# Copying reciprocal rows between SBUF partitions with four transfers instead of through a DRAM row

## The chip, the cores and the metric

The kernel runs on one core of a Trainium2 chip. The metric is the device time of one execution, in microseconds (us). The kernel before takes 621.2 us (median of 3, 618.96 to 623.64).

The engines are named as the profile names them: PE (TensorE matmul), PEld (its weight loads), DVE (VectorE), ACT (ScalarE), POOL (GpSimd), SP (SyncE). SPq and ACTq are the issues of transfers by SP and ACT.

## The reference

Causal attention with a decay by forget gates, followed by a feed-forward layer with SiLU:

```python
# q, k, v: (8, 8, 576, 64) f32; f: (8, 8, 576); w_in: (512, 2048); w_out: (2048, 512)
scores = q @ k^T / 8 + (cum_i - cum_j)        # cum = cumsum(log(clip(f, 1e-4, 1)))
attn   = softmax(scores with causal mask)
x      = (attn @ v), heads side by side       # (4608, 512)
h      = x @ w_in
out    = (h * sigmoid(h)) @ w_out             # (4608, 512) f32
```

## The kernel before

A "unit" is one pair of heads of one batch: 32 units, each with S = 576 queries. Per unit, PE transposes q and k (tp, copied by DVE to qkT), makes transposed scores (sc), ACT takes the exponential (u), and DVE masks it. Two sums over the keys follow: the numerator (nm, 64 partitions for each head) and the denominator (dn). To save PE and DVE time, the denominator is computed for two units (four heads) at once, 32 partitions for each head, and one reciprocal on DVE serves all four. The numerator needs the reciprocal on 64 partitions for each head, so rows have to be copied across partitions. That copy is the subject:

```python
    def den(qd):                      # for units 2*qd and 2*qd + 1
        dn = psc.tile([P, 1024], FP32, name="dn", tag="sc")
        ...                           # matmuls: head j on partitions 32j to 32j+31, all 32 rows equal
        rec = recp.tile([P, S], FP32, name="rec", tag="rec")
        nc.vector.reciprocal(out=rec[:, :], in_=dn[:, 0:S])
        row = drow.tile([4, S], FP32, name="row", tag="row")          # in DRAM
        nc.sync.dma_start(out=row[:, :], in_=rec[0:P:32, :])
        for m in range(2):
            rb = rbp.tile([P, S], FP32, name="rb", tag="rb")
            nc.sync.dma_start(
                out=rb[:, :],
                in_=row[2 * m : 2 * m + 2, None, :].to_broadcast([2, D, S]),
            )
            recs[2 * qd + m] = rb

    def num(n):
        ...                           # matmuls: nm, 64 partitions for each head
        rb = recs.pop(n)
        nc.vector.tensor_tensor(
            out=xT[:, p, b * S : (b + 1) * S], in0=nm[:, 0:S], in1=rb[:, :], op=ALU.mult
        )
```

The feed-forward layer is cut into tasks of four matmuls of 512 columns, hp (first layer; ACT tanh and DVE gt follow) and po (second layer), and `fill(k)` puts k of them between the attention steps to keep PE busy. `finished(n)` allows the hp tasks that need the outputs up to unit n:

```python
    for n in range(NU):
        scores(n, 0); fill(1); ...; scores(n, 1); fill(1); scores(n, 2); fill(2)
        if n % 2 == 0 and n >= 2:
            den(n // 2 - 1)
            fill(2)
        if n % 2 == 1 and n >= 3:
            num(n - 3)
            fill(1)
            num(n - 2)
            finished(n - 2)
            fill(1)
        if n + 1 < NU:
            transposes(n + 1)
        fill(2)
```

While DVE waits for rb before it can write xT, it does nothing else in these traces (the timeline below shows it idle for 5.15 and 5.26 us before two xT). The qkT copy and the gt work that come after xT on DVE wait too, and so does PE: tp, sc, dn and nm share two PSUM buffers, and the one that holds nm is free again only when xT has been written (PE's tp waits 45.4 us for xT in all, below). The pairs of units alternate: around one reciprocal the fills are mostly po, around the next mostly hp (the prediction calls them po half and hp half).

The softmax here doesn't subtract the row's maximum and nothing guards it: scores larger than these inputs give would overflow.

## Time and profile before

| | before |
|---|---|
| time, median | 621.2 us |
| span of the profiled run | 618.5 us |
| PE busy, and idle (span less busy) | 421.5, 197.0 us |
| DVE, ACT busy | 232.1, 203.4 us |
| mean granted PE clock | 0.885 |

No engine is busy all the time. First, of the page's part 4, the chain of work that ended last, by engine and by line:

```profile
DMA 46%; PE 22%; DVE 12%; issue 10%; ACT 4%; POOL 3%; SPq 1%; DVEq 0%; POOLq 0%; ACTq 0%
DMA rb<-row 37%; PE po L371 9%; PE hp L344 9%; DVE rec L294 7%; DMA row<-rec 5%; ACT u L241 3%; DMA qkb<-in_q_dram 3%; POOL qkb L71 2%; PE sc L234 2%; DVE gt L353 2%; PE tp L197 1%; SPq L299 1%; DVE xT L326 1%; DMA qkb<-in_k_dram 1%; PE dn 
```

Second, the waits: who waited for what, in total us, how often, and the longest.

```profile
DVE xT L326 <- DMA rb<-row: 191.5, 32, 26.1
...
PE hp L344 <- DVE xT L326: 68.4, 16, 5.9
...
PE sc L234 <- DVE qkT L203: 49.2, 19, 6.4
...
PE tp L197 <- DVE xT L326: 45.4, 7, 25.3
```

Every one of the 32 units waits for its rb on DVE, and PE's three largest waits are for things that DVE writes. Third, the timeline of one such stall (each `...` marks lines left out; start in us, duration, engine, line, operation, output<-inputs, count, and in brackets the idle time before it and what ended it):

```profile
220.45 3.76 DVE L294 RECIPROCAL rec<-dn 128x576 f32<-128x576 f32 x1 [0.98 <-PE dn L286]
220.56 1.67 PE L371 MATMUL po<-w_out_bf,gt 128*128 128x512 bf16 x7 [0.16 <-issue]
...
224.24 0.54 SPq L296 DMA_DIRECT2D row<-rec  x1
...
225.99 1.10 SPq L299 DMA_DIRECT2D rb<-row  x2
...
231.67 0.86 PE L314 MATMUL nm<-u,vp 128*64 128x512 bf16 x16
...
232.60 0.60 PE L344 MATMUL hp<-xT,w_in_bf 128*128 128x512 bf16 x2
...
234.96 0.76 DVE L326 TENSOR_TENSOR xT<-nm,rb 128x576 bf16<-128x576 f32 x1 [5.15 <-DMA rb<-row]
235.77 0.38 PE L344 MATMUL hp<-xT,w_in_bf 128*128 128x512 bf16 x1 [2.56 <-DVE xT L326]
...
240.97 0.76 DVE L326 TENSOR_TENSOR xT<-nm,rb 128x576 bf16<-128x576 f32 x1 [5.26 <-DMA rb<-row]
241.79 0.59 PE L344 MATMUL hp<-xT,w_in_bf 128*128 128x512 bf16 x1 [5.64 <-DVE xT L326]
...
242.16 1.50 PE L197 MATMUL tp<-ident_bf,qkb 128*128 128x128 bf16 x10
...
244.00 3.19 PE L344 MATMUL hp<-xT,w_in_bf 128*128 128x512 bf16 x7 [0.34 <-issue]
```

The reciprocal ends at 224.2. From the issue of the row to that of the first rb it takes 1.75 us. Both rb transfers are issued by 227.1, but DVE can use the first at 234.96 and the second only at 240.97. PE was through with num at 232.7. After the stall PE is slow as well: 7 hp matmuls take 3.19 us, where 7 po matmuls took 1.67 us at 220.56.

Last, one stretch of the view by windows, in which almost nothing but rb moves; the last two columns are the DMA share and GB/s:

```profile
core 0: us, PE busy (x) PEld busy (x) DVE busy (x) ACT busy (x) POOL busy (x), PEclk, DMA share, GB/s
460.50:473.00 12.50, 9.96 (x82) 4.62 (x80) 4.78 (x9) 4.71 (x9) 0.00 (x0) 1.00 0.13 47
```

A share of 0.13 of sixteen engines comes to 2.1: rb takes as much engine time as two of the sixteen have.

### The profile page before, as it was taken

To read this page: it belongs to the slowest core of one execution; us is meant where nothing else is said; L and a number is where in the kernel's file an instruction comes from. 1 tells how busy PE (TensorE), PEld (TensorE's weight loads), DVE (VectorE), ACT (ScalarE), POOL (GpSimd) and SP (SyncE) were. 2 spreads that over 40 slices of the span, in tenths; PEclk is the share of its full clock that TensorE was granted. 3 is DMA by queue.
4 is the path that set the end of the run, shared out by engine and by line. 5 is a ranking of instruction groups with operands and counts; after the bars stand their busy time and mean duration, and the time that the engine had idled before them with its cause. 6 is when DMAs were issued, how large, how long until landed. Compare 5 with 4: busy or idle time off the path is not lost.

```text
span 618.5 us, 7337 instructions
## 1 busy us (share of the span) xinstructions
PE 421.5 (68%) x2966; PEld 184.2 (30%) x3013; DVE 232.1 (38%) x337; ACT 203.4 (33%) x312; POOL 118.2 (19%) x154
## 2 busy tenths in 40 slices
PE   0461033977678594868596785859486948939997
PEld 0231021432233141323232242424232413414443
DVE  1440041743246132724165133713272328406430
ACT  2240021532245131712254233613172317105431
POOL 8738213130305003410305011500000000000000
PEclk9999997887969596977879697979799969978999
DMA  9999943291239114561329110911101110120011
GB/s 148 132 164 191 126 97 83 38 100 29 95 72 89 35 55 121 39 74 39 100 50 97 36 69 22 85 36 57 46 13 45 50 41 13 52 83 1 17 52 68
DMA packets 126705, 42.71 MB, mean 69 GB/s; under 512 B 113744, under 2 KB 117840, under 8 KB 126672
## 3 DMA queue, kind: packets, MB, share of 16 engines
q0 software_dynamic: 79392, 13.64, 28.8%
q1 hardware_dynamic: 47280, 28.61, 16.8%
q8 instruction: 23, 0.38, 0.3%
q14 instruction: 10, 0.08, 0.1%
HBM read 46.28 MB, written 9.58 MB: 90 GB/s over the span
## 4 chain that ended last, share of the span: by engine, by line
DMA 46%; PE 22%; DVE 12%; issue 10%; ACT 4%; POOL 3%; SPq 1%; DVEq 0%; POOLq 0%; ACTq 0%
DMA rb<-row 37%; PE po L371 9%; PE hp L344 9%; DVE rec L294 7%; DMA row<-rec 5%; ACT u L241 3%; DMA qkb<-in_q_dram 3%; POOL qkb L71 2%; PE sc L234 2%; DVE gt L353 2%; PE tp L197 1%; SPq L299 1%; DVE xT L326 1%; DMA qkb<-in_k_dram 1%; PE dn L286 1%
## 5 line engine op out<-in xcount | busy, mean ns | idle before, releaser
L344 PE MATMUL hp<-xT,w_in_bf 128*128 128x512 bf16 x553 | 151.9, 407 | 71.5 <-DVE xT L326 68.4
L241 ACT ACTIVATE u<-sc 128x1024 bf16<-128x1024 f32 x96 | 97.3, 1027 | 182.2 <-PE sc L234 139.7
L371 PE MATMUL po<-w_out_bf,gt 128*128 128x512 bf16 x552 | 149.5, 412 | 3.6 <-issue 2.9
L352 ACT ACTIVATE th<-hp 128x512 bf16<-128x512 f32 x144 | 86.9, 604 | 162.7 <-PE hp L344 157.2
L353 DVE SCALAR_TENSOR_TENSOR gt<-th,hp 128x512 bf16<-128x512 bf16 x144 | 95.8, 681 | 66.9 <-ACT th L352 66.9
L326 DVE TENSOR_TENSOR xT<-nm,rb 128x576 bf16<-128x576 f32 x32 | 24.3, 758 | 191.5 <-DMA rb<-row 191.5
L344 PEld LDWEIGHTS <-w_in_bf 128*128 128x128 bf16 x576 | 52.6, 102 | 97.9 <-issue 53.4
L234 PE MATMUL sc<-qkT 64*128 64x512 bf16 (+4 forms) x320 | 44.1, 351 | 53.4 <-DVE qkT L203 49.2
L371 PEld LDWEIGHTS <-gt 128*128 128x128 bf16 x576 | 53.5, 103 | 68.1 <-issue 20.0
L197 PE MATMUL tp<-ident_bf,qkb 128*128 128x128 bf16 (+1 forms) x320 | 40.3, 259 | 45.7 <-DVE xT L326 45.4
L294 DVE RECIPROCAL rec<-dn 128x576 f32<-128x576 f32 x16 | 60.1, 3754 | 6.3 <-PE dn L286 6.3
L197 PEld LDWEIGHTS <-qkb 128*128 128x128 bf16 (+1 forms) x320 | 27.5, 113 | 106.2 <-issue 97.3
L71 POOL DMA_DIRECT2D qkb<-in_q_dram x45 | 38.9, 864 | 97.9 <-PE tp L197 91.3
L254 DVE TENSOR_TENSOR u<-u,mask 128x768 bf16<-128x768 bf16 x32 | 17.9, 558 | 77.7 <-ACT u L241 77.7
L380 ACT ACTIVATE osb<-po 128x512 f32<-128x512 f32 x36 | 21.5, 597 | 63.3 <-PE po L371 46.4
L234 PEld LDWEIGHTS <-qkT 64*128 64x128 bf16 x320 | 12.0, 101 | 99.2 <-DVE qkT L203 60.9
L71 POOL DMA_DIRECT2D qkb<-in_k_dram x45 | 38.5, 855 | 11.4 <-DMA w_in_bf<-in_moe_w_in_dram 5.0
L314 PE MATMUL nm<-u,vp 128*64 128x64 bf16 (+4 forms) x512 | 30.0, 264 | 0.2
L203 DVE COPY qkT<-tp 128x1152 bf16<-128x1152 bf16 x32 | 23.6, 738 | 9.5 <-PE tp L197 9.5
L314 PEld LDWEIGHTS <-vp 128*64 128x64 bf16 x512 | 20.1, 117 | 17.9 <-issue 12.7
L286 PE MATMUL dn<-u,w_bf 128*32 128x64 bf16 (+4 forms) x512 | 14.8, 261 | 0.2
L286 PEld LDWEIGHTS <-w_bf 128*32 128x32 bf16 (+1 forms) x576 | 10.9, 100 | 10.8 <-issue 6.4
(73 smaller groups left out, 106.5 us busy)
## 6 DMA issues: line engine op xcount, KB each, us to landing
rb<-row SPq DMA_DIRECT2D x32, 288.0 KB
out_dram<-osb SPq DMA_DIRECT2D x36, 256.0 KB
qkb<-in_q_dram POOLq DMA_DIRECT2D x28, 128.0 KB, 6.6
qkb<-in_k_dram POOLq DMA_DIRECT2D x28, 128.0 KB, 12.9
w_in_bf<-in_moe_w_in_dram POOLq DMA_DIRECT2D x4, 512.0 KB, 10.3
w_out_bf<-in_moe_w_out_dram POOLq DMA_DIRECT2D x4, 512.0 KB, 10.7
qkb<-in_q_dram POOLq DMA_DIRECT2D x15, 64.0 KB, 6.0
qkb<-in_k_dram POOLq DMA_DIRECT2D x15, 64.0 KB, 6.6
```

Of the source, the lines that this page charges most:

```text
L71: nc.gpsimd.dma_start(out=qkb[b][:n, i, c, h0 * D : h1 * D].rearrange("p (h d) -> p h d", d=D), in_=src[b, h0:h1, c * P : c * P + n, :].re ...
L197: nc.tensor.transpose(tp[:, i, c * P : c * P + nk], src[:nk, i, c, p * P : (p + 1) * P], ident_bf[:nk, :nk],)
L234: nc.tensor.matmul(sc[:, i, col : col + q1 - q0], lhsT=t[r, 1, kb * P : (kb + 1) * P], rhs=t[r, 0, q0:q1], start=True, stop=True,)
L241: nc.scalar.activation(out=u[:, :, c * 512 : (c + 1) * 512], in_=sc[:, :, :], func=ACT.Exp, scale=scale)
L286: nc.tensor.matmul(dn[32 * j : 32 * j + 32, q0:q1], lhsT=w_bf[r, kb, bh : bh + 1].to_broadcast([nk, 32]), rhs=rhs, start=(kb == 0), stop=( ...
L294: nc.vector.reciprocal(out=rec[:, :], in_=dn[:, 0:S])
L314: nc.tensor.matmul(nm[i * D : (i + 1) * D, q0:q1], lhsT=v_t[r, p, :] if kb == NM else vp[:, kb, 2 * p + i, :], rhs=(ut[r, :] if kb == NM e ...
L326: nc.vector.tensor_tensor(out=xT[:, p, b * S : (b + 1) * S], in0=nm[:, 0:S], in1=rb[:, :], op=ALU.mult)
L344: nc.tensor.matmul(hp[:, :], lhsT=w_in_bf[:, cc, fc * P : (fc + 1) * P], rhs=xT[:, cc, t0 : t0 + TG], start=(cc == 0), stop=(cc == NCC - 1),)
L352: nc.scalar.activation(out=th[:, :], in_=hp[:, :], func=ACT.Tanh, scale=0.5)
L353: nc.vector.scalar_tensor_tensor(out=gt[:, fc, :], in0=th[:, :], scalar=1.0, in1=hp[:, :], op0=ALU.add, op1=ALU.mult,)
L371: nc.tensor.matmul(po[:, :], lhsT=gt[:, fc, tb * P : (tb + 1) * P], rhs=w_out_bf[:, fc, :], start=(fc == 0), stop=(fc == NFC - 1),)
```

## The change

The intent is to drop the DRAM row and to copy the reciprocals inside SBUF: the 32 equal rows of a head go twice, to fill its 64 partitions. The call of `finished` moves behind the next fill. The diff is complete:

```diff
-    drow = ctx.enter_context(tc.tile_pool(name="drow", bufs=3, space=bass.MemoryType.DRAM))
@@ den
         nc.vector.reciprocal(out=rec[:, :], in_=dn[:, 0:S])
-        row = drow.tile([4, S], FP32, name="row", tag="row")
-        nc.sync.dma_start(out=row[:, :], in_=rec[0:P:32, :])
         for m in range(2):
             rb = rbp.tile([P, S], FP32, name="rb", tag="rb")
-            nc.sync.dma_start(
-                out=rb[:, :],
-                in_=row[2 * m : 2 * m + 2, None, :].to_broadcast([2, D, S]),
-            )
+            for i in range(2):
+                j = 2 * m + i
+                for h in range(2):
+                    nc.sync.dma_start(
+                        out=rb[i * D + 32 * h : i * D + 32 * h + 32, :],
+                        in_=rec[32 * j : 32 * j + 32, :],
+                    )
             recs[2 * qd + m] = rb
@@ main loop
             num(n - 2)
+            fill(1)
             finished(n - 2)
-            fill(1)
```

## The prediction

> **What bounds the kernel now.** No engine: the page shows PE busy 421.5 of 618.5 us, DVE 232.1, ACT 203.4. The chain of waits gives 36.8% to the transfer rb<-row and 5.1% to row<-rec. In the waits, DVE xT sits 191.5 us (32 times, every unit) for rb<-row; behind it PE hp waits 68.4 us, tp 45.4 us, and sc 49.2 us (for qkT[...]). The timeline of one pair of units: rec 220.45 to 224.2, row issued 224.24, both rb 225.99 to 227.1, xT at 234.96 and 240.97 (rb lands 9 and 15 us after issue); PE had finished num at 232.6. After the stall PE runs cold: 7 hp in 3.19 us against 8 in 1.90.
>
> **Why rb is slow.** The source of rb<-row has an outermost dimension of 2. [...] The trace agrees: with only rb in flight (460.5 to 473 us), the DMA share is 0.13 (2/16) at 47 GB/s.
>
> **The change.** It removes row<-rec (1.7 to 3 us to landing) and replaces each rb by four transfers of 32 partitions[...]. Eight issues at about 0.55 us (one SP issue as measured) cost 4.4 us of SP per pair instead of 1.6. Estimate, with 1.7 us landing as for row<-rec: first rb ready 3.9 us after rec ends, second 6.1 us (before: 10.7 and 16.8). PE reaches num about 5.5 us (po half) or 6.7 us (hp half) after rec ends and ends the second num 3 us later, so both waits vanish. Moving `finished` keeps the fill after num off the xT being written; under 1 us per pair once rb is early.
>
> **Sum.** Between the recs a pair takes 33 us; PE work from warm stretches (hp x8 1.9, tp 0.98, dn 0.94, nm 1.0) is 21 to 22 us, plus about 1.6 us in the hp-heavy half, where qkT waits behind rec and gt on DVE. I take 23 us: 12 pairs save about 120 us. Start (up to 108 us): the first two rb land at 73 and 80 us because they share saturated DMA queues (queue share over 1.3 until 73 us), and the next ones stop PE from 97 to 107; I expect 20 to 25 us saved, as the loads remain. End: last rb at 555.9 instead of about 545, and 8 us of cold clock: 13 us. Together 155 to 165 us: about 456 us.
>
> **What would show it.** rb in the waits of DVE xT falls from 191.5 to under 25 us, nearly all in the first 80 us; DMA gone from the chain, PE (hp, po) the largest share; pair period 22 to 24 us; PEclk near 1.0 in the middle; PE busy about 370 us; DVE work (gt behind rec) the new largest wait.
>
> **What would make it wrong.** [...] v loads and output stores ahead of rb issues could hold them (out stores wait 251.7 us for osb already). Issue may cost more than 0.55 us. The order on DVE, ACT, SP may be built differently. The start may save nothing. DVE may stop PE more at the denser pace.
>
> Predicted 456 us, 8 in 10 between 436 and 490; faster by over 2%: 0.97, same 0.02, slower 0.01.

Two were about the order of work on DVE and SP; what a trace shows of it is that in after the copies are issued from 48.5 us on, behind a v load issued at 48.1, though the first reciprocal ended at 42.0. The "8 us of cold clock" are in the trace of before: from 556.7 to 565.0 us the granted PE clock is 0.68, then 1.00.

## The result, and the profile after

The kernel after takes 457.38 us (median of 4, 456.47 to 457.59); before in the same comparison 622.07 (4 runs). The ratio is 0.7354, 95% interval 0.7323 to 0.7386. Ratios here and below are the mean time of one kernel's fast runs over that of the other's of the same rounds, so not quite the ratio of the medians.

The chain, and the waits that answer to those of before (most lines have moved by one; L326 is still xT):

```profile
PE 48%; DMA 13%; issue 12%; DVE 11%; ACT 7%; SPq 4%; POOL 4%; DVEq 0%; POOLq 0%; ACTq 0%
PE po L371 27%; PE hp L344 10%; DMA rb<-rec 8%; ACT u L240 6%; DVE gt L353 5%; PE nm L314 4%; DMA qkb<-in_q_dram 4%; SPq L299 4%; PE sc L233 3%; DVE rec L293 3%; POOL qkb L70 3%; PE tp L196 3%; PE dn L285 1%; DMA qkb<-in_k_dram 1%; ACT th L
```

```profile
PE sc L233 <- DVE qkT L202: 26.9, 16, 4.0
...
DVE xT L326 <- DMA rb<-rec: 23.9, 8, 13.8
...
PE tp L196 <- DVE xT L326: 13.1, 1, 13.1
...
PE hp L344 <- DVE xT L326: 0.8, 1, 0.8
```

DVE's wait for rb falls from 191.5 to 23.9 us, of which 13.8 are one wait in the start. PE's wait for xT falls from 68.4 + 45.4 to 13.9 us, again nearly all in the start. The same stretch of work in the timeline:

```profile
250.29 3.76 DVE L293 RECIPROCAL rec<-dn 128x576 f32<-128x576 f32 x1 [0.83 <-PE dn L285]
...
254.07 5.18 SPq L299 DMA_DIRECT2D rb<-rec  x8
...
259.60 0.86 PE L314 MATMUL nm<-u,vp 128*64 128x512 bf16 x16
...
260.65 0.76 DVE L326 TENSOR_TENSOR xT<-nm,rb 128x576 bf16<-128x576 f32 x1 [0.79 <-PE nm L314]
261.51 0.86 PE L314 MATMUL nm<-u,vp 128*64 128x512 bf16 x16
...
262.56 0.76 DVE L326 TENSOR_TENSOR xT<-nm,rb 128x576 bf16<-128x576 f32 x1 [1.15 <-PE nm L314]
263.32 0.98 PE L196 MATMUL tp<-ident_bf,qkb 128*128 128x128 bf16 x10
...
264.46 1.67 PE L344 MATMUL hp<-xT,w_in_bf 128*128 128x512 bf16 x7 [0.16 <-issue]
```

Eight issues take 5.2 us, and now xT waits for PE (nm), not for a transfer. PE goes on without a gap and at its full pace (7 hp in 1.67 us). The view of the tile rb gives the median time from issue to landing of a copy as 2.1 us (1.9 to 10.9).

Where the 164.2 us of span went is read by stage. A stage ends where the same PE instruction starts in both traces (tp of the seventh unit; tp of the 31st), or with the last xT. The first column is the stretch, the second its length, then busy us of PE and others, PE clock, DMA share (it adds up the time of all packets, so it can exceed 1), GB/s:

```profile
0.00:108.10 108.10, 31.89 (x284) 17.49 (x286) 26.21 (x47) 21.85 (x28) 55.08 (x80) 0.97 1.13 134
108.10:504.10 396.00, 292.79 (x2127) 123.43 (x2161) 160.24 (x228) 140.55 (x216) 63.11 (x74) 0.85 0.38 60
504.10:556.70 52.60, 39.69 (x310) 18.07 (x315) 23.62 (x30) 17.15 (x28) 0.00 (x0) 0.89 0.12 43
556.70:618.50 61.80, 57.14 (x248) 25.25 (x252) 22.00 (x32) 23.90 (x40) 0.00 (x0) 0.94 0.09 35
```

```profile
0.00:80.00 80.00, 30.39 (x281) 16.94 (x281) 26.39 (x46) 21.96 (x28) 50.01 (x74) 1.00 1.45 164
80.00:354.00 274.00, 257.30 (x2127) 115.80 (x2162) 160.67 (x229) 138.80 (x215) 68.45 (x80) 1.00 0.64 91
354.00:395.20 41.20, 38.88 (x315) 17.90 (x319) 23.66 (x30) 17.74 (x29) 0.00 (x0) 1.00 0.20 57
395.20:454.30 59.10, 54.50 (x248) 24.65 (x252) 22.02 (x32) 23.91 (x40) 0.00 (x0) 0.98 0.11 39
```

The start gives 28.1 us, the twelve pairs of units in the middle 122.0 (396.0 to 274.0, that is 33.0 to 22.8 us per pair), the last pairs 11.4, the end 2.7. Seen from PE: the busy time of the same instructions falls from 421.5 to 381.1 us, 40.4 us, and idle time from 197.0 to 73.2 us, 123.8 us. The stalls thus cost about a third again of their length in slow matmuls after them. In the stall shown above, after the idle time of 5.64 us, 7 hp took 3.19 us and not 1.67, and PE was slow from 241.79 to about 247.7, some 5.9 us.

### The profile page after: what moved, and what is told of

Same layout as the page of the kernel before. It is cut to its first block, busy times and chain, and to the rows that moved or that the text cites. A ratio compares the mean times of both kernels' runs of the same rounds, so it can differ in the third digit from the quotient of the medians.

```text
span 454.3 us, 7436 instructions
## 1 busy us (share of the span) xinstructions
PE 381.1 (84%) x2966; PEld 175.3 (39%) x3013; DVE 232.7 (51%) x337; ACT 202.4 (45%) x312; POOL 118.5 (26%) x154
## 4 chain that ended last, share of the span: by engine, by line
PE 48%; DMA 13%; issue 12%; DVE 11%; ACT 7%; SPq 4%; POOL 4%; DVEq 0%; POOLq 0%; ACTq 0%
PE po L371 27%; PE hp L344 10%; DMA rb<-rec 8%; ACT u L240 6%; DVE gt L353 5%; PE nm L314 4%; DMA qkb<-in_q_dram 4%; SPq L299 4%; PE sc L233 3%; DVE rec L293 3%; POOL qkb L70 3%; PE tp L196 3%; PE dn L285 1%; DMA qkb<-in_k_dram 1%; ACT th L352 1%
## 5 line engine op out<-in xcount | busy, mean ns | idle before, releaser
L344 PE MATMUL hp<-xT,w_in_bf 128*128 128x512 bf16 x551 | 136.8, 380 | 2.9 <-issue 1.1
L371 PE MATMUL po<-w_out_bf,gt 128*128 128x512 bf16 x554 | 134.3, 380 | 2.6 <-issue 2.1
L371 PEld LDWEIGHTS <-gt 128*128 128x128 bf16 x576 | 50.8, 98 | 59.0 <-issue 5.2
L344 PEld LDWEIGHTS <-w_in_bf 128*128 128x128 bf16 x576 | 49.9, 98 | 58.9 <-issue 7.5
L233 PE MATMUL sc<-qkT 64*128 64x512 bf16 (+4 forms) x320 | 40.6, 325 | 31.9 <-DVE qkT L202 26.9
L326 DVE TENSOR_TENSOR xT<-nm,rb 128x576 bf16<-128x576 f32 x32 | 24.2, 756 | 45.0 <-DMA rb<-rec 23.9
L196 PE MATMUL tp<-ident_bf,qkb 128*128 128x128 bf16 (+1 forms) x320 | 34.5, 231 | 13.3 <-DVE xT L326 13.1
L196 PEld LDWEIGHTS <-qkb 128*128 128x128 bf16 (+1 forms) x320 | 24.3, 102 | 28.8 <-issue 15.4
L285 PEld LDWEIGHTS <-w_bf 128*32 128x32 bf16 (+1 forms) x576 | 10.9, 100 | 10.8 <-issue 6.4
## 6 DMA issues: line engine op xcount, KB each, us to landing
w_out_bf<-in_moe_w_out_dram POOLq DMA_DIRECT2D x4, 512.0 KB, 11.4
```

What stands on the lines that cost most here:

```text
L196: nc.tensor.transpose(tp[:, i, c * P : c * P + nk], src[:nk, i, c, p * P : (p + 1) * P], ident_bf[:nk, :nk],)
L233: nc.tensor.matmul(sc[:, i, col : col + q1 - q0], lhsT=t[r, 1, kb * P : (kb + 1) * P], rhs=t[r, 0, q0:q1], start=True, stop=True,)
L326: nc.vector.tensor_tensor(out=xT[:, p, b * S : (b + 1) * S], in0=nm[:, 0:S], in1=rb[:, :], op=ALU.mult)
L344: nc.tensor.matmul(hp[:, :], lhsT=w_in_bf[:, cc, fc * P : (fc + 1) * P], rhs=xT[:, cc, t0 : t0 + TG], start=(cc == 0), stop=(cc == NCC - 1),)
L371: nc.tensor.matmul(po[:, :], lhsT=gt[:, fc, tb * P : (tb + 1) * P], rhs=w_out_bf[:, fc, :], start=(fc == 0), stop=(fc == NFC - 1),)
```

## The experiments

Three theories stood at the start. **A**: an rb transfer runs on about 2 of the 16 engines (0.13 of them by its DMA share), because its source has an outermost (slowest) dimension of 2; the number of engines is the whole cost. **B**: the trip through DRAM is the cost, and SBUF as source is what helps. **C**: PE stalls because the fill after num needs the xT just written, and the move of `finished` is what helps. That the count goes with the dimension was the assumption at this point, which the runs test. Eleven kernels were run; all are correct. The traces show no engine count of a transfer, only DMA share and landing time; where a share was read it stands beside the count.

### finished_only: before, with finished moved

```diff
             num(n - 2)
+            fill(1)
             finished(n - 2)
-            fill(1)
```

> The kernel before with only the later call of finished. Theory A (the transfer rb<-row runs on 2 of 16 engines and that is the whole cost): 612 to 624 us, within 2% of before, DVE xT still waits about 190 us for rb<-row. Rival C (PE stalls because the fill after num needs the xT just written): under 600 us.

Measured: 613.15 us, ratio 0.9856 (0.9828 to 0.9883).

```profile
DVE xT L326 <- DMA rb<-row: 187.7, 30, 25.5
PE tp L197 <- DVE xT L326: 64.0, 14, 25.0
PE hp L344 <- DVE xT L326: 35.9, 9, 5.4
```

The wait for rb stays (187.7 us). PE waits 32.5 us less in hp and 18.6 us more in tp: most of the stall is only met at another instruction. C is worth 8 us in the kernel before and does not explain the change.

### copies_only: after, with finished back in its old place

```diff
             num(n - 2)
-            fill(1)
             finished(n - 2)
+            fill(1)
```

> The kernel after with finished back in its old place: the four transfers alone. Theory A: 455 to 468 us, PE hp waits for DVE xT some 0 to 1 us per pair of units, up to 10 us in all. Rival C: at least 490 us.

Measured: 457.48 us, ratio 0.7369 (0.7342 to 0.7396), against 0.7354 for the whole change. The copies alone are the whole effect. The 8 us of the move are gone here, as it hides part of a stall that no longer exists (PE hp waits for xT for 1.4 us in all).

### dram_k16, dram_k8, dram_k4: the DRAM row kept, the outermost dimension larger

Each head's row is written several times (32 equal rows are there to take from), so that a transfer's source can have 4, 8 or 16 rows outermost. There are still one write and two read transfers for each pair of units. For 16, with finished moved as in after:

```diff
-        row = drow.tile([4, S], FP32, name="row", tag="row")
-        nc.sync.dma_start(out=row[:, :], in_=rec[0:P:32, :])
+        row = drow.tile([32, S], FP32, name="row", tag="row")
+        nc.sync.dma_start(out=row[:, :], in_=rec[0:P:4, :])
@@
-                in_=row[2 * m : 2 * m + 2, None, :].to_broadcast([2, D, S]),
+                in_=row[16 * m : 16 * m + 16, None, :].to_broadcast([16, 8, S]),
```

(For 8: 16 rows, rec[0:P:8], [8, 16, S]. For 4: 8 rows, rec[0:P:16], [4, 32, S].)

> The DRAM row is kept, but written with each head's row 8 times (32 rows) so that the source of each rb transfer has an outermost dimension of 16; finished moved as in after; still one write and two reads per pair of units. Theory A (engine count): 452 to 470 us, DVE xT waits under 35 us for rb. Rival B (the trip through DRAM is the cost): above 560 us, xT still waits over 120 us.

> As the run before, with each head's row twice (8 rows), outermost dimension 4. Theory A: each rb takes about 3.5 us instead of 7, so the second rb lands about 11 us after rec ends, some 2 us after PE needs it: 465 to 510 us. Rival B: above 560 us, equal to the variant of 16 within 2%.

> DRAM row with each head's row 4 times, outermost dimension 8. Theory A: rb transfers take half of the time of the variant of 4 (501 us), both land before PE has finished num: 461 to 475 us, close to the variant of 16 (462.4).

| outermost dimension | 2 (before) | 2 (finished_only) | 4 | 8 | 16 | after (SBUF) |
|---|---|---|---|---|---|---|
| median, us | 621.2 | 613.15 | 501.01 | 471.51 | 462.39 | 457.38 |
| ratio to before | 1 | 0.9856 | 0.8061 | 0.7578 | 0.7443 | 0.7354 |
| DVE xT waits for rb, us | 191.5 | 187.7 | 99.2 | 44.5 | 29.2 | 23.9 |

All three lie in A's range. One part of the text for 8 missed: there DVE still waits for rb in 16 units (11 in the variant of 16), so not every rb lands before PE has finished num. The variant of 16 has everything that B blames, the write to DRAM, the wait for it and the reads, and is 1% from after. In its middle it is not slower at all: from one reciprocal to that ten pairs later it takes 227.3 us (120.15 to 347.45), where after takes 227.7 (113.27 to 340.94). Its 5 us are in the start, where PE's seventh-unit tp comes at 86.6 instead of 80.0 us. So B is worth about 1%, and in these two traces only in the start.

The variant of 4 also shows the size. In a pair without loads, the second xT comes 9.0 us after the issue of the two transfers (343.07 to 352.06), where before it was 14.7 us (362.26 to 376.94). An estimate from these two: taking a fixed part f and a part that falls with the outermost dimension d as w/d, f + w/2 = 14.7 and f + w/4 = 9.0 give f = 3.3 and w = 22.8 us.

The DMA share, where little but rb moves, follows the outermost dimension: 0.13 with 2 (above), 0.24 with 4 (413 to 419 us, 82 GB/s), 0.48 with 8 (364.2 to 365.0 us, 138 GB/s), which is 2.1, 3.8 and 7.7 of sixteen engines. For 16 no share was read; there an rb lands 3.9 us after its issue in the median (3.3 to 8.3). These views also answer a rival: with fewer copies of a row in DRAM, each is read more often (64 times before, 32 with 4, 16 with 8), and that could itself be slow. Then an engine would move less where a row is read more often. It does not: GB/s divided by 16 times the share is 22.6, 21.4 and 18.0 (an estimate from these views).

### sbuf_31: SBUF copies as in after, but one of two cut into 31 and 1 partitions

```diff
-                for h in range(2):
+                for d0, d1 in ((0, 32), (32, 63), (63, 64)):
                     nc.sync.dma_start(
-                        out=rb[i * D + 32 * h : i * D + 32 * h + 32, :],
-                        in_=rec[32 * j : 32 * j + 32, :],
+                        out=rb[i * D + d0 : i * D + d1, :],
+                        in_=rec[32 * j + d0 % 32 : 32 * j + d0 % 32 + d1 - d0, :],
```

> SBUF source as in after, no DRAM row, but of each head's two 32-partition copies the second is cut into 31 and 1 partitions[...]. Theory A: an rb then has 2 x 31 rows x 2304 B = 143 KB on one engine, about what each of the two engines carried before (147 KB, 6 to 7 us); the second rb is there about 15 us after rec ends: 560 to 620 us, xT waits over 130 us for rb. Rival B (SBUF instead of DRAM is what helps): 455 to 470 us.

A copy of 31 partitions should load about one engine. That was the assumption; the share below is what the run shows of it.

Measured: 576.62 us, ratio 0.9270 (0.9234 to 0.9307). This is the test from the other side, with no DRAM row and the same bytes; only one of every two copies of 32 partitions became 31 + 1. The waits, and one window while such copies run:

```profile
DVE xT L326 <- DMA rb<-rec: 150.3, 30, 21.3
```

```profile
130.00:138.00 8.00, 5.76 (x24) 2.15 (x24) 2.62 (x4) 1.01 (x1) 0.00 (x0) 0.79 0.08 23
```

A DMA share of 0.08 comes to 1.3 of sixteen engines, and 119 of the some 164 us that the change gave are lost again (576.62 - 457.38). Four more issues for each pair are part of it (in the middle 12 issues took 7.9 to 10.5 us; in after 8 took 5.0 to 6.2). How large a part, one pair without loads shows: the second xT comes 15.8 us after the first issue (268.38 to 284.14). The last copy of after lands about 7.3 us after it (an estimate: 5.2 of issues and 2.1 to landing), and the issues explain 2.9 of these 8.5 us. B is refuted as the main cause: with SBUF as source, most of the gain is lost again (119 of 164 us) if half of each rb is copied in 31 and 1 partitions, at that share.

### den_unit: no copies at all

The denominator is computed for one unit on 64 partitions per head, so that the reciprocal falls where it is used. The edit in outline (the rest of the matmul's arguments is as before):

```diff
-        dn[32 * j : 32 * j + 32, q0:q1], lhsT=w_bf[r, kb, bh : bh + 1].to_broadcast([nk, 32])  # one dn for 4 heads
-        nc.vector.reciprocal(out=rec[:, :], in_=dn[:, 0:S]);  8 copies to rb
+        for m in range(2):        # one dn for each unit
+            dn[i * D : (i + 1) * D, q0:q1], lhsT=w_bf[r, kb, bh : bh + 1].to_broadcast([nk, D])
+            nc.vector.reciprocal(out=rb[:, :], in_=dn[:, 0:S])
```

> No copies at all: the denominator is computed per unit on 64 partitions for each head, so the reciprocal lands where it is used. Adds 16 reciprocals of 3.76 us on DVE (60 us, DVE 232 to 292) and 16 den passes of 0.93 us on PE (15 us). If the copies of after are hidden in the middle, this costs more than it saves at the start (13 us): 460 to 490 us. If the copies still cost in the middle: under 450 us.

Measured: 500.64 us, ratio 0.8049 (0.8019 to 0.8078). The direction was as expected, since in the middle the copies are nearly free, but I missed the size by at least 10 us. Beside the added DVE and PE work, PE waits for the reciprocals themselves:

```profile
PE sc L233 <- DVE qkT L202: 37.6, 19, 4.0
...
PE tp L196 <- DVE rb L293: 22.7, 15, 2.5
```

Two dn tiles fill both PSUM buffers that tp needs, and DVE takes 7.37 us for both reciprocals. I had not counted that. But its start was better: the first hp matmul came at 74.5 instead of 81.3 us.

### start_act and late_wout: why the first copies are late

In after, the first reciprocal ends at 42.0 us, its copies are issued from 48.5 us on, and the first xT comes at 60.86 us. Two kernels asked why. In the first, the copies of the first two pairs are issued on ACT's queue; in the second, the load of w_out is asked for six steps later.

```diff
-                    nc.sync.dma_start(
+                    (nc.scalar if qd < 2 else nc.sync).dma_start(
```

```diff
-            if p == 1 and b == 0:
+            if p == 3 and b == 1:
                 for i in range(WQ):
                     load_w_out(i)
```

> After, but the rb copies of the first two pairs are issued on the ACT queue. In after they are issued at 48.5 us, behind a v load in the SP queue, though rec ended at 42.0, and their 8 issues take 11 us. If the SP order is what delays the start: first rb lands at 48 to 52 instead of 60.9 us and the time falls to 442 to 452 us. If the full DMA queues are what delays it: 454 to 459 us.

> After, with the load of w_out asked for six steps later (the build puts two of its four parts before and two after the next q and k loads). PE, DVE and ACT have the same order. If the first rb copies are late because the DMA queues are full at 42 to 66 us: issue of the first 8 copies takes less than 11 us, first xT before 58 us instead of 60.9, time 450 to 456 us. If not: 456 to 459 us, first xT at 60 to 62 us.

Both missed. start_act took 468.87 us (ratio 0.7539, 0.7512 to 0.7565), slower than after. The issues began at 42.0 as hoped; the chain of waits shows what followed:

```profile
50.57 16.27 DMA vf<-in_v_dram
...
66.86 6.00 DMA rb<-rec
```

Six of the eight copies were issued by 49.2 us, but the last two only at 64.4 and 66.9 us, after v loads (vf) had landed. ACT could not go on until then, and the exponentials of the fourth unit, ready since 43 us, ran at 67.4. In after, the eighth copy waits 6.1 us for a v load in the same way, but on SP, which has only transfers to issue. The trace doesn't say why the program makes these issues wait for a load. Issuing from ACT made the issues begin at 42.0 instead of 48.5 us, while the median time to landing of all copies stayed at 2.1 us; and ACT, which has work of its own, paid for the issues that had to wait (its exponentials started 29.9 us after its work before).

late_wout took 462.46 us (ratio 0.7445, 0.7419 to 0.7471). It doesn't test what it was meant to. The build moved only half of the load, POOL freed the v buffers earlier, and six v loads got ahead of the copies in SP's order, so that these were issued at 54.9 us, and the first xT came at 64.6. This points to the order on SP, but the moved load is in it too. In the trace of after, 6.5 us pass from the end of the reciprocal to the first issue, as SP first waits to issue a v load, and about 10 from the fourth issue (the first rb is then complete in the queue) to the first xT, at a DMA share of 1.39 between 48 and 62 us. How much the start would gain from a better order alone, and how much from emptier queues, stays open.

### hybrid2 and hybrid2_late: no copies in the start, copies in the middle

den_unit's start joined to after's middle:

```diff
     def den(qd):
+        if qd < 2:
+            ...        # as in den_unit: one dn and one reciprocal for each unit, no copies
+            return
```

> After, but the first two pairs of units take the denominator per unit on 64 partitions per head (no copies there; DVE and PE are idle then), and the other 14 pairs the copies. In den_unit the first hp matmul came at 74.5 us, in after at 81.3; the middle should be as in after: 447 to 453 us, faster than after (457.4) by 1 to 2%. If the start is bound by the loads whatever rb does: 455 to 459 us.

> Both changes of this call. With no copies at the start the late w_out should not help further: within 1% of hybrid2, 445 to 455 us.

Measured: hybrid2 448.98 us, ratio 0.7230 (0.7207 to 0.7252); with the late w_out 451.37 us, ratio 0.7268 (0.7245 to 0.7290). hybrid2 beats after, whose ratio to before was 0.7354 (0.7323 to 0.7386); 0.7230 / 0.7354 is 1.7% less time (through the kernel before; the two did not run in the same rounds). Both lie in the ranges expected. hybrid2 is the fastest kernel. The reason is the start: its seventh-unit tp comes at 72.5 instead of 80.0 us, and the rest takes 375.2 us against 374.3 in after.

```profile
37.88 7.37 DVE L294 RECIPROCAL rb<-dn 128x576 f32<-128x576 f32 x2
...
51.73 1.41 DVE L353 TENSOR_TENSOR xT<-nm,rb 128x576 bf16<-128x576 f32 x2
```

The first xT comes at 51.73 us instead of 60.86, and waits for no transfer.

## Why the prediction was right

- **Total.** Predicted 456 us (436 to 490), measured 457.38.
- **Cause.** Right, and now shown from both sides: a larger outermost dimension with the DRAM row kept (DMA share 0.13, 0.24, 0.48 with 2, 4, 8) brings the gain (462.39 with 16), and a lower share with the row gone (0.08) takes most of it away (576.62).
- **Middle.** Predicted 23 us for a pair and about 120 us in all; measured 22.8 and 122.0.
- **Start.** Predicted 20 to 25 us; measured 28.1. The fifth unit's tp comes 12.5 us earlier (61.67 instead of 74.15), and from there to the seventh's it takes 15.6 us less (80.02 - 61.67 against 108.11 - 74.15). The term was sized too small: PE's stall of 9.4 us before the seventh unit went as foretold, but the first two rb also came earlier than expected (xT at 60.9 and 65.7 instead of 73.3 and 80.5 us), though the loads were still running.
- **End.** Predicted 13 us; measured 11.4 + 2.7 = 14.1.
- **Copies.** Predicted 4.4 us for eight issues and 1.7 us to landing; measured 5.0 to 6.2 us in the middle (median issue 0.588 us) and 2.1 us. In the hp half of pairs with loads, the second rb is therefore up to 2.0 us late for DVE. PE does not notice: there, PE's only wait from 105 to 385 us for anything that DVE writes is sc<-qkT, 12.0 us in 9 times, mostly the 1.7 us of the hp half that the prediction named.
- **Signs.** xT's wait for rb under 25 us: 23.9, but only about 16 in the first 80 us. PE clock near 1: 0.998. PE busy about 370 us: 381.1; in the start PE still runs slow (10 tp take 1.45 to 1.48 us, in the middle 0.98). Two signs were wrong as worded. DMA did not leave the chain: it keeps 13%, 8% for rb<-rec, as in five pairs the late second rb (6.3 to 7.4 us each) lies on the chain that ended last, though PE does not wait for it. And gt behind rec did not become the largest wait of the page; it is only the largest left to PE in the middle.
- **finished.** Put at under 1 us per pair, once rb is early; measured as nothing (457.48 without it).

## What to carry to other kernels

Look at the outermost dimension of a transfer's source, not only at its bytes: a broadcast with 2 outermost had a DMA share of 0.13 here, 2.1 of 16 engines, and a changed access pattern of the row and its reads, with the row still in DRAM (and finished moved, as in after), brought 97% of the gain ((621.46 - 462.39) of (621.46 - 457.48) us). When many engines are half idle, find the wait that repeats in every step of the loop, then ask what else stands behind it in the same queue: a wait on DVE here cost PE its idle time (123.8 us) and then its pace (40.4 us more for the same instructions, at a granted clock of 0.885 instead of 0.998). A fix that only moves work around a stall (here finished) can gain alone (8 us) and be worth nothing once the stall is gone.

## Further numbers of this case

- Two 288 KB broadcasts took 14.7 us from issue to DVE's use of the second with an outermost dimension of 2 (share 0.13, 47 GB/s) and 9.0 us with 4; the kernel took 613, 501, 472 and 462 us with 2, 4, 8 and 16.
- For each pair of units, eight transfers of 72 KB beat two of 288 KB with 2 outermost (457.4 against 621.2 us) and did no worse than two of 288 KB with 16 outermost (462.4).
- The issue of one copy on SP took 0.51 us at least and 0.59 in the median (in after), and could wait for an earlier load to land (6.1 us on SP in after; up to about 15 us on ACT in start_act, which stopped ACT). Whether chip or build makes it wait is not shown here.
- A copy of 72 KB inside SBUF landed in 2.1 us in the median (1.9 to 10.9).
- In after, one granted clock goes with two paces: 16 nm matmuls at 46.9 us took 1.49 us, against 0.86 us at 259.6, while the view by windows shows 1.00 for both stretches.
